# Three banks for transposed scores, three for projections, and the half-sums' addition one maximum later

## The chip, the cores and the metric

One core of a Trainium2 chip runs the kernel. The metric is the time of one execution on the device in microseconds (us). The engines have the profile's names: PE is TensorE (matmuls), PEld its loading of weights, DVE is VectorE, ACT is ScalarE, POOL is GpSimd, and SP issues the DMA transfers. TensorE writes its results to PSUM, which holds eight banks of 128 partitions x 512 fp32 values.

## The reference

Input x is 2048 tokens x 512. The result mixes an attention A and a gated layer B, token by token:

```python
g = sigmoid((x * gate_w).sum(-1, keepdims=True))
a = attention(x)      # 32 heads of 16; query q sees keys q-255 .. q; then @ wo
b = (sigmoid(x @ w_gate) * (x @ w_up)) @ w_down    # 512 -> 1376 -> 512
return g * a + (1 - g) * b
```

All of it is fp32 with random inputs. The kernel holds each factor of a large matmul as a high and a low part, so such a product is three matmuls.

## The kernel before

**Work in units.** The attention is cut into 128 units: 8 groups of 4 heads x 16 blocks of 128 tokens. The main loop (`for u in range(N)`, N = 140) does for each step u, and in it for each head hh of four:

- `s_part(u, hh)`, L306: the scores of a query block against its keys (a matmul to a PSUM bank of tag `s`), of which VectorE takes the row maximum at L312 (tile names `junk`, `mx`).
- `st_part(u - 9, hh)`, L353: the transposed scores of a unit nine steps back, with the maximum already taken off (a bank of tag `st`), of which ScalarE takes the exponential into a slot of `region` (L358). The unit's slot is u % 7 of seven slots of 1536 values.
- `run_slots(GAP)`: three slots of the projections, `gu` (the gated layer's two inputs) and `pj` (queries and keys of later groups), L238. Each group of 12 matmuls sums in one bank of tag `misc`, as two halves of 64 rows of the contraction, one on each half of the array; the second half runs 19 slots behind. When a group is done, ScalarE copies its bank out (`sp` at L494, `pr` at L250).
- Two lists of small jobs, `behind` (for VectorE, subtractions for low parts) and `acts` (for ScalarE): one job of each is popped per head, after that head's `s_part` and `st_part`.

**Bursts.** Every fourth step begins with a burst, `pv_burst` (L382): the exponentials of four query blocks times the values, small matmuls at L405, one half of the rows into a bank of tag `s` (`pvs`), the other into one of tag `st` (`pvst`). `o_take` adds the two half-sums: ScalarE copies `pvs` to `ob` (L419), VectorE adds `pvst` (L420). For the query blocks of units 120 to 127 the bursts are of two blocks.

**Banks.** The eight banks are two of tag `s`, two of tag `st` and four of tag `misc`. A tile takes the next bank of its tag in turn and waits until that one's last reader is done.

**Order.** Each engine runs its instructions in the order in which the code issues them; semaphores hold the engines together. So the order of the code around `s_part`, `st_part`, the pops and the slots is what sets the order of the work.

**Stages.** First the splits, the values and the first projections (to about 97 us); then the main loop with scores (to about 552 us); the tail, u from 128 to 139, with no scores left and six slots between its heads (to about 601 us); then the second phase: the gated layer's second matmul (`pd`, L77 to L79, in the four banks of tags `s` and `st`) and the attention's last projection (`pa`, tag `misc`). The gated layer's inputs went to DRAM as they were made (`gu_scratch`). `h_load(n)`, L567, loads step n's two raw pieces back into one of seven slots at the end of `region`, and `h_skew` turns them into the high and low parts `hb`, two or three steps ahead of `pd`. The loads of steps 0 to 4 are issued in the tail by the table HLOAD, at u = 135 (0), 136 (1), 137 (2 and 3) and 138 (4); from step 5 on, load n + 5 is issued in step n.

Of the kernel before, what the change touches and what calls it, by code (L numbers as in the profile page):

```python
# [7 lines left out]
F32 = mybir.dt.float32  # L8
# [25 lines left out]
REGION = PR * PW  # L34
NHV = 7
HV0 = REGION - NHV * 2 * CH
BURST = 4
# [17 lines left out]
def gated_mix_kernel(  # L55
# [70 lines left out]
    with ExitStack() as actx:  # L126
# [51 lines left out]
        nc.vector.memset(warm[:, 0:2 * P].bitcast(F32), 0.0)  # L178
        warm_ps = ps.tile([P, CH], F32, tag="st", name="warm_ps", bufs=2)
        for _ in range(16):  # L180
# [40 lines left out]
        def v_part(b, d):  # L221
            if d == 0:
                vp[b] = ps.tile([P, D], F32, tag="misc", name=f"vps{b}", bufs=4)
            bs = slice(b * P, (b + 1) * P)
            mm3(vp[b], xh[:, d, bs], xl[:, d, bs], wvh[:, d], wvl[:, d], d == 0, d == ND - 1)
            if d == ND - 1:
                nc.scalar.copy(Vh[:, b, :, 0:DH], vp.pop(b).rearrange("p (h w) -> p h w", w=DH))
                later.append((v_d[b], V[:, b]))
# [13 lines left out]
        def proj_mm(s, k, half=None):  # L242
            g, c = divmod(s, NC)
            if s not in pj:
                pj[s] = ps.tile([P, CH], F32, tag="misc", name=f"pj{s}", bufs=4)
            group_mm(pj[s], P, *wq[g], c, k, half)
# [49 lines left out]
        def s_part(u, hh):  # L296
# [5 lines left out]
            tag = "st" if u < LAG and hh >= 2 else "s"  # L302
            pt = ps.tile([P, 3 * P], F32, tag=tag, name=f"s{u}_{hh}", bufs=2)
            lhsT = blk(g, i, hh, 0)
# [39 lines left out]
        def st_part(u, hh):  # L344
            g, j = divmod(u, NB)
            if u not in pts:
                o = u % PR * PW
                pts[u] = region[:, o:o + PW].rearrange("p (h q) -> p h q", h=HG)
            pt = ps.tile([P, 3 * P], F32, tag="st", name=f"st{u}_{hh}", bufs=2)
            lhsT = blk(g, j, hh, 1)  # L350
# [32 lines left out]
        def pv_burst(u, n):  # L383
            g, i = divmod(u, NB)
            acc = [
                ps.tile([P, CH], F32, tag=tag, name=f"pv{tag}{u}", bufs=2) for tag in ("s", "st")
            ]
# [25 lines left out]
        def o_take(g, i, n, acc):  # L413
# [5 lines left out]
            nc.scalar.copy(part, acc[0][:, 0:n * P])  # L419
            nc.vector.tensor_tensor(part[:, lo:], acc[1][:, lo:n * P], part[:, lo:], op=ALU.add)  # L420
            if (i + n) % 4:
                return
            ob, c = obs.pop(s), i // 4
            for hh in range(HG):
                h = g * HG + hh
                later.append((oT_d[h * DH:(h + 1) * DH, c * CH:(c + 1) * CH], ob[32 * hh:32 * hh + DH]))
            later.append((sum_d[c, g * HG:(g + 1) * HG], ob.rearrange("(h r) f -> r h f", r=32)[DH]))

# [56 lines left out]
        def gu_mm(f, c, w, k, half=None):  # L485
            fw = width(f, w)
            if (f, c, w) not in gp:
                gp[f, c, w] = ps.tile([P, CH], F32, tag="misc", name=f"gu{f}_{c}_{w}", bufs=4)
            group_mm(gp[f, c, w], fw, gv[:, 0, w, :, 0:fw], gv[:, 1, w, :, 0:fw], c, k, half)
# [71 lines left out]
        steps = [(c, f) for c in range(NC) for f in range(NF)]  # L561
        hv = region[:, HV0:].rearrange("p (n w t) -> p n w t", w=2, t=CH)

        def h_load(n):
            c, f = steps[n]
            for w in range(2):
                nc.sync.dma_start(hv[0:FCH[f], n % NHV, w], gu_d[w, f, 0:FCH[f], c * CH:(c + 1) * CH])  # L567

        def h_skew(n):
            a, b = n + 2, n + 3  # L570
            if 0 <= a < len(steps):
                fw = FCH[steps[a][1]]
                hts[a] = cpool.tile([P, CH2], F32R, tag="hb", name=f"hb{a}", bufs=4)
                src = hv[0:fw, a % NHV, 1]
                split(hts[a][0:fw, 0:CH], hts[a][0:fw, CH:], src)
            if 0 <= b < len(steps):
                fw = FCH[steps[b][1]]
                tg, tu = hv[0:fw, b % NHV, 0], hv[0:fw, b % NHV, 1]
                nc.scalar.activation(tg, tg, AF.Sigmoid)
# [29 lines left out]
        U_LAST = 4 * (NSTEP - 2 - 5)  # L609
        HLOAD = {N - 5: [0], N - 4: [1], N - 3: [2, 3], N - 2: [4]}  # L610
        WD = NU - 5
# [10 lines left out]
        for u in range(N):  # L622
            if u == LAG:
                vctx.close()
                ppool = actx.enter_context(tc.tile_pool(name="ppool", bufs=1))
                for k in range(2):
                    vg.append(ppool.tile([P, NB * GW + 16], F32, name=f"vg{k}"))
                    nc.gpsimd.memset(vg[k][:, NB * GW:], 0.0)
            if u == LAG + 1 or u % NB == 0 and 0 < u < NU:
                v_load(u // NB)  # L630
# [69 lines left out]
            if SUMS + 2 <= u and (u - SUMS) % 4 == 2:  # L700
                behind.append(lambda c=(u - SUMS) // 4: later.append(sums_invert(c)))
            for n in HLOAD.get(u, ()):
                h_load(n)
            if u >= N - 2:
# [17 lines left out]
        def free_slot(h, d, c):  # L722
# [10 lines left out]
        spare = [  # L733
            region[:, 3 * CH * k:3 * CH * (k + 1)].rearrange("p (n t) -> p n t", t=CH) for k in range(2)
        ]
# [31 lines left out]
        for n, (c, f) in enumerate(steps):  # L767
# [10 lines left out]
            if f == 0:  # L778
                pd = [
                    ps.tile([P, D], F32, tag="s" if t < 2 else "st", name=f"pd{4 * c + t}", bufs=2)  # L780
                    for t in range(4)
# [25 lines left out]
            for t in range(4):  # L807
                b = 4 * c + t
                acc = accs[b % len(accs)]
                nc.scalar.activation(acc, pd[t], AF.Copy, scale=omg[:, b:b + 1])  # L810
                pa = ps.tile([P, D], F32, tag="misc", name=f"pa{b}", bufs=4)
                for d in range(ND):
# [57 lines left out]
```

## Time and profile before

| | us |
|---|---|
| median of three runs | 774.91 |
| the three runs | 773.41, 774.91, 775.33 |
| the profiled execution | 775.56 |
| its span in the trace | 773.9 |
| mean granted TensorE clock in it | 0.995 of full speed |

The runs and the profiled execution are times of whole executions; the trace's span runs from its first instruction to its last. In the views that follow, a group of rows has a line of the kernel, an engine, an operation and its tiles (`out<-in`); a wait's row says which engine and line waited for which other, how long in all, how often, and the longest. A row of the timeline is start, duration, engine, line, operation, tiles and shapes, and in brackets how long the engine stood idle before it and what ended that.

### The profile page before, as it was taken

To read this page: it belongs to the slowest core of one execution; us is meant where nothing else is said; L and a number is where in the kernel's file an instruction comes from. 1 tells how busy PE (TensorE), PEld (TensorE's weight loads), DVE (VectorE), ACT (ScalarE), POOL (GpSimd) and SP (SyncE) were. 2 spreads that over 40 slices of the span, in tenths; PEclk is the share of its full clock that TensorE was granted. 3 is DMA by queue.
4 is the path that set the end of the run, shared out by engine and by line. 5 is a ranking of instruction groups with operands and counts; after the bars stand their busy time and mean duration, and the time that the engine had idled before them with its cause. 6 is when DMAs were issued, how large, how long until landed. Compare 5 with 4: busy or idle time off the path is not lost.

```text
span 773.9 us, 20559 instructions
## 1 busy us (share of the span) xinstructions
PE 753.5 (97%) x7652; PEld 609.2 (79%) x7652; DVE 485.5 (63%) x1429; ACT 437.4 (57%) x900; POOL 163.4 (21%) x256
## 2 busy tenths in 40 slices
PE   8999999999999999999999999999999999999998
PEld 6877778877887877888787788888876778888886
DVE  5346767766676766766677676567511794839381
ACT  5412666666576656666667666665764663625341
POOL 7000323233133232323313323232331000000000
PEclk8999999999999999999999999999999999999999
DMA  8363544445444454444544425542346785648351
GB/s 292 97 207 130 142 130 127 121 108 160 120 125 116 123 146 133 116 109 123 149 130 113 127 68 158 150 143 79 111 128 206 230 275 192 212 147 258 105 165 54
DMA packets 88787, 112.69 MB, mean 146 GB/s; under 512 B 36082, under 2 KB 45810, under 8 KB 88688
## 3 DMA queue, kind: packets, MB, share of 16 engines
q1 hardware_dynamic: 88688, 111.39, 49.2%
q8 instruction: 60, 0.98, 0.5%
q14 instruction: 39, 0.32, 0.1%
HBM read 49.72 MB, written 36.45 MB: 111 GB/s over the span
## 4 chain that ended last, share of the span: by engine, by line
PE 84%; DVE 9%; DMA 3%; issue 2%; ACT 1%; SPq 1%; DVEq 0%; ACTq 0%
PE gu L238 32%; PE pvs L405 8%; PE pj L238 7%; PE s L306 6%; PE st L353 5%; PE pd L79 4%; PE pd L77 4%; PE pd L78 4%; DVE junk L312 3%; PE vps L77 2%; PE vps L78 2%; PE vps L79 2%; PE pa L77 2%; PE pa L79 2%; PE pa L78 2%
## 5 line engine op out<-in xcount | busy, mean ns | idle before, releaser
L238 PE MATMUL gu<-xh,w 64*128 64x512 f32 (+3 forms) x1384 | 357.3, 395 | 0.0
L312 DVE CUSTOM_DVE_ANT_0 junk<-s,mask 128x384 f32<-128x384 f32 (+2 forms) x512 | 271.1, 530 | 90.9 <-PE s L306 40.9
L358 ACT ACTIVATE region<-st 128x384 f32<-128x384 f32 (+2 forms) x512 | 238.6, 474 | 129.7 <-PE st L353 77.4
L238 PE MATMUL gu<-xl,w 64*128 64x512 f32 (+3 forms) x692 | 237.1, 394 | 0.0
L238 PEld LDWEIGHTS gu<-xh,w 64*128 64x128 f32 (+3 forms) x1384 | 206.5, 183 | 12.9 <-issue 0.2
L306 PE MATMUL s<-ring 64*128 64x384 f32 (+2 forms) x536 | 165.6, 333 | 9.8 <-DVE mx L312 9.5
L353 PE MATMUL st<-ring 64*128 64x384 f32 (+2 forms) x536 | 172.4, 338 | 2.1 <-DVE ob L420 1.3
L363 POOL TENSOR_SCALAR_AFFINE_SELECT region<-region 128x512 f32<-128x512 f32 x128 | 82.6, 646 | 368.2 <-ACT region L358 356.8
L306 PEld LDWEIGHTS s<-ring 64*128 64x128 f32 x536 | 94.1, 184 | 41.4 <-DVE mx L312 31.7
L238 PEld LDWEIGHTS gu<-xl,w 64*128 64x128 f32 (+3 forms) x692 | 116.8, 183 | 7.0 <-issue 1.6
L353 PEld LDWEIGHTS st<-ring 64*128 64x128 f32 x536 | 97.3, 184 | 18.1 <-DVE ob L420 11.7
L238 PE MATMUL pj<-xh,wqh 64*128 64x512 f32 (+1 forms) x232 | 94.4, 409 | 1.5 <-ACT xh L73 1.5
L238 PE MATMUL pj<-xl,wqh 64*128 64x512 f32 (+1 forms) x232 | 91.4, 398 | 0.4 <-DVE xl L74 0.2
L420 DVE TENSOR_TENSOR ob<-pvst,ob 128x512 f32<-128x512 f32 (+2 forms) x34 | 21.9, 645 | 100.9 <-ACT ob L419 82.8
L405 PE MATMUL pvs<-region,vg 64*32 64x320 f32 (+4 forms) x1440 | 74.5, 346 | 0.0
L238 PE MATMUL pj<-xh,wql 64*128 64x512 f32 (+1 forms) x232 | 73.2, 402 | 0.0
L405 PE MATMUL pvst<-region,vg 64*32 64x320 f32 (+4 forms) x1440 | 73.1, 341 | 0.0
L368 POOL TENSOR_SCALAR_AFFINE_SELECT region<-region 128x512 f32<-128x512 f32 x112 | 71.5, 638 | 0.0
L79 PE MATMUL pd<-ring,hb 128*128 128x512 f32 (+1 forms) x176 | 69.4, 394 | 0.9 <-DVE hb L74 0.9
L405 PEld LDWEIGHTS pvs<-region,vg 64*32 64x32 f32 x1440 | 49.7, 106 | 25.9 <-issue 9.5
L77 PE MATMUL pd<-ring,hb 128*128 128x512 f32 (+1 forms) x176 | 69.5, 395 | 0.3 <-ACT hb L73 0.3
L78 PE MATMUL pd<-ring,hb 128*128 128x512 f32 (+1 forms) x176 | 68.8, 391 | 0.4 <-DVE ring L119 0.4
(72 smaller groups left out, 1011.3 us busy)
## 6 DMA issues: line engine op xcount, KB each, us to landing
gu_scratch<-sp SPq DMA_DIRECT2D x80, 256.0 KB
region<-gu_scratch SPq DMA_DIRECT2D x80, 256.0 KB
ring<-sh SPq DMA_DIRECT2D x128, 128.0 KB
ring<-sl SPq DMA_DIRECT2D x64, 128.0 KB
guraw<-in_wgu_dram SPq DMA_DIRECT2D x20, 256.0 KB
v_scratch<-region SPq DMA_DIRECT2D x16, 272.0 KB
vg<-v_scratch SPq DMA_DIRECT2D x8, 544.0 KB
region<-in_xT_dram SPq DMA_DIRECT2D x16, 256.0 KB
```

Source lines behind the costliest of these rows:

```text
L77: mm(ps, lh, rh, start=first, stop=False)
L78: mm(ps, lh, rl, start=False, stop=False)
L79: mm(ps, ll, rh, start=False, stop=last)
L238: mm(pt[0:fw], (wl if w == 2 else wh)[r, d], (xl if w == 1 else xh)[r, d, c * CH:(c + 1) * CH], start=k == 0 and half != 1, stop=k == 3 * ...
L306: mm(pt[:, (k - k0) * P:(e - k0) * P], lhsT, blk(g, k, hh, 1, e - k), start=k == k0, stop=e == i + 1, skip_group_check=True,)
L312: nc.vector.tensor_tensor_reduce(junk[:, 0:n], pt[:, 0:n], mask[:, 3 * P - n:], scale=1.0, scalar=NEG, op0=ALU.add, op1=ALU.max, accum_out ...
L353: mm(pt[:, (q - j) * P:(e - j) * P], lhsT, blk(g, q, hh, 0, e - q), start=q == j, stop=e == last, skip_group_check=True,)
L358: nc.scalar.activation(pts[u][:, hh, 0:n], pt[:, 0:n], AF.Exp, scale=SCALE)
L363: nc.gpsimd.affine_select(p[:, :, 0:P], p[:, :, 0:P], pattern=[[0, HG], [1, P]], compare_op=ALU.is_ge, fill=0.0, base=0, channel_multiplie ...
L368: nc.gpsimd.affine_select(p[:, :, 2 * P:], p[:, :, 2 * P:], pattern=[[0, HG], [-1, P]], compare_op=ALU.is_gt, fill=0.0, base=0, channel_mu ...
L405: mm(acc[half][32 * hh:32 * hh + 32, q0:q1], vg[g % 2][r, c:c + 32], pts[g * NB + j][r, hh, q0 + o:q1 + o], start=m == 0, stop=m == len(or ...
L420: nc.vector.tensor_tensor(part[:, lo:], acc[1][:, lo:n * P], part[:, lo:], op=ALU.add)
```

## The change

**Banks.** Tag `st` has three banks, tag `misc` three, tag `s` two as before. The tiles of the start, `vps`, `pj`, `gu`, `pa`, `pd` and the warm-up are counted alike.

**The addition.** In `o_take`, VectorE's addition of `pvst` and the issue of the finished `ob` are put into a function `rest`, which goes to the front of `behind`. It is popped after the first head's `s_part` and `st_part` of the same step.

**Raw pieces.** The seven slots of the second phase's raw pieces are no longer the end of `region`: the first is the front of `vg0` (the values' buffer of the even groups), the others lie at six fixed places in `region` (HVO). The exponentials of the last seven units take slots 2, 3, 6, 0, 1, 2, 3 (PSLOT), so that they don't lie there. Loads 0 to 4 are issued at u = 130, 132, 134, 136 and 138. Buffers of the second phase that were at the front of `region` move by SPARE.

```diff
-NHV = 7
-HV0 = REGION - NHV * 2 * CH
+PSLOT = [w % PR for w in range(121)] + [2, 3, 6, 0, 1, 2, 3]
+HVO = [6144, 7168, 8192, 9216, 0, 1024]
+SPARE = 3072
+NHV = len(HVO) + 1
...
-                pj[s] = ps.tile([P, CH], F32, tag="misc", name=f"pj{s}", bufs=4)
+                pj[s] = ps.tile([P, CH], F32, tag="misc", name=f"pj{s}", bufs=3)
...
-            pt = ps.tile([P, 3 * P], F32, tag=tag, name=f"s{u}_{hh}", bufs=2)
+            pt = ps.tile([P, 3 * P], F32, tag=tag, name=f"s{u}_{hh}", bufs=2 if tag == "s" else 3)
...
-                o = u % PR * PW
+                o = PSLOT[u] * PW
...
-            pt = ps.tile([P, 3 * P], F32, tag="st", name=f"st{u}_{hh}", bufs=2)
+            pt = ps.tile([P, 3 * P], F32, tag="st", name=f"st{u}_{hh}", bufs=3)
...
-                ps.tile([P, CH], F32, tag=tag, name=f"pv{tag}{u}", bufs=2) for tag in ("s", "st")
+                ps.tile([P, CH], F32, tag=tag, name=f"pv{tag}{u}", bufs=bufs)
+                for tag, bufs in (("s", 2), ("st", 3))
...
             nc.scalar.copy(part, acc[0][:, 0:n * P])
-            nc.vector.tensor_tensor(part[:, lo:], acc[1][:, lo:n * P], part[:, lo:], op=ALU.add)
-            if (i + n) % 4:
-                return
-            ob, c = obs.pop(s), i // 4
...
+            def rest():
+                nc.vector.tensor_tensor(part[:, lo:], acc[1][:, lo:n * P], part[:, lo:], op=ALU.add)
+                if (i + n) % 4:
+                    return
+                ob, c = obs.pop(s), i // 4
...
+            behind.insert(0, rest)
...
-                gp[f, c, w] = ps.tile([P, CH], F32, tag="misc", name=f"gu{f}_{c}_{w}", bufs=4)
+                gp[f, c, w] = ps.tile([P, CH], F32, tag="misc", name=f"gu{f}_{c}_{w}", bufs=3)
...
-        HLOAD = {N - 5: [0], N - 4: [1], N - 3: [2, 3], N - 2: [4]}
+        HLOAD = N - 2 * AHEAD
...
+                hvs += [
+                    v.rearrange("p (w t) -> p w t", t=CH)
+                    for v in [vg[0][:, 0:2 * CH]] + [region[:, o:o + 2 * CH] for o in HVO]
+                ]
...
-            for n in HLOAD.get(u, ()):
-                h_load(n)
+            if u >= HLOAD and (u - HLOAD) % 2 == 0:
+                h_load((u - HLOAD) // 2)
...
-                    ps.tile([P, D], F32, tag="s" if t < 2 else "st", name=f"pd{4 * c + t}", bufs=2)
+                    ps.tile([P, D], F32, tag="s" if t < 2 else "st", name=f"pd{4 * c + t}", bufs=2 + t // 2)
...
-                pa = ps.tile([P, D], F32, tag="misc", name=f"pa{b}", bufs=4)
+                pa = ps.tile([P, D], F32, tag="misc", name=f"pa{b}", bufs=3)
```

VectorE's instructions around the burst of step 54 (its half-sums are `pvst40`, named for the first query block's unit), before; a `junk` row is the maximum of the score that it names:

```order
L312 ISA junk53_3_3970,mx13_3863<-s53_3_3968,mask_155 128x384
L312 ISA mx13_3863 128x1
L420 TENSOR_TENSOR ob10_4028<-pvst40_3979,ob10_4028 128x512
L312 ISA junk54_0_4037,mx13_3863<-s54_0_4035,mask_155 128x384
L312 ISA mx13_3863 128x1
L312 ISA junk54_1_4050,mx13_3863<-s54_1_4048,mask_155 128x384
```

The same place in the changed kernel:

```order
L314 ISA junk53_3_3970,mx13_3863<-s53_3_3968,mask_155 128x384
L314 ISA mx13_3863 128x1
L314 ISA junk54_0_4036,mx13_3863<-s54_0_4034,mask_155 128x384
L314 ISA mx13_3863 128x1
L425 TENSOR_TENSOR ob10_4028<-pvst40_3979,ob10_4028 128x512
L314 ISA junk54_1_4050,mx13_3863<-s54_1_4048,mask_155 128x384
```

The addition stands behind the first maximum of its step and not in front of it; nothing else on VectorE changes places.

TensorE's order is the same in both, but not what its instructions wait for. Behind the same burst, before, with the engine in brackets for which an instruction waits (`s54_1` is the second score of step 54, `st45_0` the second transposed score, `gu3_3_0`, `gu3_2_0` and `gu3_0_1` are projection groups):

```order
L353 MATMUL st45_0_4052<-ring_63 128x384 [waits DVE_49]
L238 MATMUL gu3_3_0_3961<-xl_71,w0_72 128x512
L238 MATMUL gu3_2_0_3901<-xh_70,w0_72 128x512
...
L306 MATMUL s54_3_4074<-ring_63 128x384 [waits DVE_49]
L353 MATMUL st45_2_4078<-ring_63 128x384 [waits Activation_49]
L238 MATMUL gu3_0_1_4081<-xh_70,w0_72 128x512
```

And in the changed kernel:

```order
L355 MATMUL st45_0_4052<-ring_63 128x384
L240 MATMUL gu3_3_0_3961<-xl_71,w0_72 128x512
L240 MATMUL gu3_2_0_3901<-xh_70,w0_72 128x512
...
L308 MATMUL s54_3_4074<-ring_63 128x384 [waits DVE_49]
L355 MATMUL st45_2_4078<-ring_63 128x384 [waits PE_49]
L240 MATMUL gu3_0_1_4081<-xh_70,w0_72 128x512 [waits Activation_49]
```

The second transposed score of the step no longer waits for VectorE, and a projection group's first matmul waits for ScalarE, which copies out the group three before it.

More of the change, by code (lines that the diff above doesn't have):

```diff
@@ L178, in gated_mix_kernel @@
         nc.vector.memset(warm[:, 0:2 * P].bitcast(F32), 0.0)
-        warm_ps = ps.tile([P, CH], F32, tag="st", name="warm_ps", bufs=2)
+        warm_ps = ps.tile([P, CH], F32, tag="st", name="warm_ps", bufs=3)
         for _ in range(16):
@@ L222, in v_part @@
             if d == 0:
-                vp[b] = ps.tile([P, D], F32, tag="misc", name=f"vps{b}", bufs=4)
+                vp[b] = ps.tile([P, D], F32, tag="misc", name=f"vps{b}", bufs=3)
             bs = slice(b * P, (b + 1) * P)
@@ L419, in o_take @@
             nc.scalar.copy(part, acc[0][:, 0:n * P])
-            nc.vector.tensor_tensor(part[:, lo:], acc[1][:, lo:n * P], part[:, lo:], op=ALU.add)
-            if (i + n) % 4:
-                return
-            ob, c = obs.pop(s), i // 4
[L424 to L427, printed above, removed]
+            def rest():
[3 more added lines that the diff above has]
+                ob, c = obs.pop(s), i // 4
+                for hh in range(HG):
+                    h = g * HG + hh
+                    later.append((oT_d[h * DH:(h + 1) * DH, c * CH:(c + 1) * CH], ob[32 * hh:32 * hh + DH]))
+                later.append((sum_d[c, g * HG:(g + 1) * HG], ob.rearrange("(h r) f -> r h f", r=32)[DH]))
+            behind.insert(0, rest)
         def proj(s):
@@ L561, in gated_mix_kernel @@
         steps = [(c, f) for c in range(NC) for f in range(NF)]
-        hv = region[:, HV0:].rearrange("p (n w t) -> p n w t", w=2, t=CH)
+        hvs = []
         def h_load(n):
@@ L566, in h_load @@
             for w in range(2):
-                nc.sync.dma_start(hv[0:FCH[f], n % NHV, w], gu_d[w, f, 0:FCH[f], c * CH:(c + 1) * CH])
+                nc.sync.dma_start(hvs[n % NHV][0:FCH[f], w], gu_d[w, f, 0:FCH[f], c * CH:(c + 1) * CH])
         def h_skew(n):
@@ L573, in h_skew @@
                 hts[a] = cpool.tile([P, CH2], F32R, tag="hb", name=f"hb{a}", bufs=4)
-                src = hv[0:fw, a % NHV, 1]
+                src = hvs[a % NHV][0:fw, 1]
                 split(hts[a][0:fw, 0:CH], hts[a][0:fw, CH:], src)
@@ L577, in h_skew @@
                 fw = FCH[steps[b][1]]
-                tg, tu = hv[0:fw, b % NHV, 0], hv[0:fw, b % NHV, 1]
+                tg, tu = hvs[b % NHV][0:fw, 0], hvs[b % NHV][0:fw, 1]
                 nc.scalar.activation(tg, tg, AF.Sigmoid)
@@ L733, in gated_mix_kernel @@
         spare = [
-            region[:, 3 * CH * k:3 * CH * (k + 1)].rearrange("p (n t) -> p n t", t=CH) for k in range(2)
+            region[:, SPARE + 3 * CH * k:SPARE + 3 * CH * (k + 1)].rearrange("p (n t) -> p n t", t=CH) for k in range(2)
         ]
```

## The prediction

> **What bounds the kernel now.** I read the page's busy times first, then the windows by stage, then the waits of the loop, then the timeline of single bursts (L382, one every four steps, about 16.2 us).
>
> The page's first part: engine, busy time, share of the span, instructions.
>
> ```profile
> PE 753.5 (97%) x7652; PEld 609.2 (79%) x7652; DVE 485.5 (63%) x1429; ACT 437.4 (57%) x900; POOL 163.4 (21%) x256
> ```
>
> The windows view for the main loop: its stretch, its length, then busy time of PE, PEld, DVE, ACT, POOL, the granted clock, the DMA share and GB/s.
>
> ```profile
> 97.00:548.00 451.00, 441.41 (x5758) 363.14 (x5758) 309.65 (x1057) 288.56 (x624) 130.22 (x210) 1.00 0.45 125
> ```
>
> TensorE lacks 451.0 - 441.4 = 9.6 us of a busy loop, at full clock. By that row it is the bound, and 9.6 us is about all that removed waits could give here. But TensorE works in two 64-row halves, and a stalled half is hidden while the other streams. The waits of the loop (97 to 552 us) show the stalls: engine, line, who is waited for, us in total, times, longest.
>
> ```profile
> PEld s L306 <- DVE mx L312: 30.3, 65, 1.3
> DVE junk L312 <- PE s L306: 28.4, 95, 0.6
> PEld st L353 <- DVE ob L420: 9.3, 29, 0.4
> PE s L306 <- DVE mx L312: 9.3, 24, 0.9
> ```
>
> The third row is what the change aims at: one wait per burst, 9.3 / 29 = 0.32 us each. The first is three times as large, and in the other direction: scores wait for VectorE to read the score before. So which of the two engines is late behind a burst? The timeline of VectorE in one period:
>
> ```profile
> 258.32 0.69 DVE L420 TENSOR_TENSOR ob<-pvst,ob 128x512 f32<-128x512 f32 x1 [2.45 <-ACT ob L419]
> 258.93 0.55 DVE L312 CUSTOM_DVE_ANT_0 junk<-s,mask 128x384 f32<-128x384 f32 x1
> 259.63 0.56 DVE L312 CUSTOM_DVE_ANT_0 junk<-s,mask 128x384 f32<-128x384 f32 x1
> 260.34 0.56 DVE L312 CUSTOM_DVE_ANT_0 junk<-s,mask 128x384 f32<-128x384 f32 x1
> 260.83 0.69 DVE L264 TENSOR_TENSOR sl<-pr,sh 128x512 fp32r<-128x512 f32 x1
> 261.43 0.55 DVE L312 CUSTOM_DVE_ANT_0 junk<-s,mask 128x384 f32<-128x384 f32 x1
> ...
> 262.84 0.56 DVE L312 CUSTOM_DVE_ANT_0 junk<-s,mask 128x384 f32<-128x384 f32 x1
> 263.60 0.56 DVE L312 CUSTOM_DVE_ANT_0 junk<-s,mask 128x384 f32<-128x384 f32 x1 [0.19 <-PE s L306]
> 264.34 0.56 DVE L312 CUSTOM_DVE_ANT_0 junk<-s,mask 128x384 f32<-128x384 f32 x1 [0.17 <-PE s L306]
> ```
>
> From the addition on, VectorE starts a maximum every 0.71 us (260.34 - 259.63) without a pause, and an addition between two costs 0.49 (260.34 to 260.83) and 0.60 (260.83 to 261.43). Real lateness shows only at 263.60, which is 263.60 - 262.84 - 0.71 = 0.05 late, and at 264.34, 0.03 late. Behind this burst TensorE costs VectorE 0.08 us, not 0.32. VectorE, 63% busy on the page, paces this stretch.
>
> **Part 1: the addition behind the next maximum, with a third st bank.** TensorE, a weight load and the release in the same place:
>
> ```profile
> 257.71 0.59 ACT L419 COPY ob<-pvs 128x512 f32<-128x512 f32 x1 [1.88 <-PE pvst L405]
> 258.15 0.33 PE L306 MATMUL s<-ring 64*128 64x384 f32 x1
> 258.79 0.33 PE L306 MATMUL s<-ring 64*128 64x384 f32 x1
> 259.07 0.18 PEld L353 LDWEIGHTS st<-ring 64*128 64x128 f32 x1 [0.32 <-DVE ob L420]
> 259.81 0.33 PE L306 MATMUL s<-ring 64*128 64x384 f32 x1
> 263.23 0.33 PE L306 MATMUL s<-ring 64*128 64x384 f32 x1
> ```
>
> Removed: the second st's load at 259.07 waits for the addition's end, 258.32 + 0.69 = 259.01, plus 0.06 to wake. With a third bank it needs no wait, since pvst's bank is not the next in turn: TensorE goes on 0.32 earlier there.
>
> Moved: the first score ends at 258.15 + 0.33 = 258.48, and a maximum starts 0.04 behind its score (263.23 + 0.33 = 263.56, then 263.60). So the first maximum starts at 258.52, the addition 0.49 behind it at 259.01, the second maximum 0.60 behind that at 259.61, where it stood at 259.63. Two operations change places in front of the same third: VectorE gains 0.02. The two instructions, their lengths and the queue behind them stay.
>
> Who is late next? The third score needs the first maximum's end to reuse its bank; before, 258.93 + 0.55 = 259.48, now 258.52 + 0.55 = 259.07. It stood at 259.81 and comes up to 0.32 earlier. The fourth needs the second maximum, which moves by 0.02 only. So TensorE's lead is caught at the fourth score, and what is left of it, 0.1 to 0.2, serves only to fill VectorE's later pauses: 0.08 + 0.02 = 0.10 us for this burst.
>
> Every second burst is followed by a step without the L264 addition, so VectorE reaches TensorE sooner. One of that kind:
>
> ```profile
> 274.42 0.69 DVE L420 TENSOR_TENSOR ob<-pvst,ob 128x512 f32<-128x512 f32 x1 [2.57 <-ACT ob L419]
> 277.15 0.56 DVE L312 CUSTOM_DVE_ANT_0 junk<-s,mask 128x384 f32<-128x384 f32 x1
> 278.02 0.56 DVE L312 CUSTOM_DVE_ANT_0 junk<-s,mask 128x384 f32<-128x384 f32 x1 [0.31 <-PE s L306]
> 278.76 0.56 DVE L312 CUSTOM_DVE_ANT_0 junk<-s,mask 128x384 f32<-128x384 f32 x1 [0.17 <-PE s L306]
> ```
>
> Here the pauses are 278.02 - 277.15 - 0.71 = 0.16 and 0.03, 0.19 in all; I take 0.16, since a lead of 0.1 to 0.2 does not fill them wholly. Mean of the kinds 0.13; 29 x 0.13 = 3.8 us. Lower bound: only the changed places, 29 x 0.02 = 0.6. Upper bound: the whole wait, 9.3.
>
> **Part 2: three banks for projections.** The group three before must now have been copied out when a group starts; before, the group four before. The copies of ScalarE and the first weight load of the third group behind, for the first and the last of 36 such starts in the loop that have under 0.4 us left (the others have more):
>
> ```profile
> 92.83 0.58 ACT L494 COPY sp<-gu 128x512 f32<-128x512 f32 x1
> 93.79 0.18 PEld L238 LDWEIGHTS gu<-xh,w 64*128 64x128 f32 x1
> ...
> 543.48 0.58 ACT L494 COPY sp<-gu 128x512 f32<-128x512 f32 x1
> 544.37 0.18 PEld L238 LDWEIGHTS gu<-xh,w 64*128 64x128 f32 x1
> ```
>
> Left: 93.79 - 93.41 = 0.38, and 544.37 - 544.06 = 0.31; minus 0.06 to wake, 0.25. TensorE's lead of up to 0.2 behind a burst eats most of it, but not all. So I take nothing in the loop; the cost if it is gone is the third rival.
>
> **The tail (u from 128 on, about 553 to 600 us)** has no scores; VectorE stands idle there, so what a st wait costs is TensorE's. The waits of that window, and a copy with the load of the third group behind it:
>
> ```profile
> PEld st L353 <- DVE ob L420: 2.4, 3, 1.0
> PEld st L353 <- ACT region L358: 1.2, 2, 0.7
> PE st L353 <- ACT region L358: 0.8, 2, 0.5
> 557.59 0.60 ACT L494 COPY sp<-gu 128x512 f32<-128x512 f32 x1
> 557.77 0.41 PEld L238 LDWEIGHTS gu<-xh,w 64*128 64x128 f32 x2
> 575.97 0.59 ACT L494 COPY sp<-gu 97x512 f32<-97x512 f32 x1
> 576.34 0.16 PEld L238 LDWEIGHTS gu<-xh,w 64*97 64x97 f32 x1
> ```
>
> Gone with the third st bank: 2.4, and of the two waits on the exponential the 0.8 that TensorE itself stands: 3.2 (bounds 2.4 and 3.6). Come in their place: the load at 557.77 must wait until 557.59 + 0.60 + 0.06 = 558.25, 0.48 us; that at 576.34 until 576.62, 0.28; between them lies one more, taken as the larger. 0.48 + 0.48 + 0.28 = 1.2, and I take 1.3 with a slot's rounding. Net -1.9 (bounds -2.4 and, if each stall is felt on both halves, 2 x 1.3 - 2.4 = +0.2).
>
> **Part 3: raw pieces in early free buffers.** Five loads of two DMAs each leave for u = 130 to 138 instead of 135 to 138, into vg0 and pieces of region that no later unit writes. SP issues them among the oT stores, the first four earlier than before, the fifth at the same step. The waits between 600 and 640 us show what they could save:
>
> ```profile
> PEld pd L79 <- DVE hb L74: 2.2, 3, 0.8
> PE pd L79 <- DVE hb L74: 0.9, 3, 0.4
> DVE region L580 <- DMA region<-gu_scratch: 2.1, 1, 2.1
> ```
>
> The one DMA wait belongs to the sixth load, which both kernels issue in the second phase. So I take 0; bounds -0.9, TensorE's share of its waits there, and +0.9, the same once more if a store is pushed behind a load.
>
> **Sum.** -3.8 - 1.9 + 0 = -5.7. The profiled execution took 775.56 us (span 773.9), 0.65 above the median of the runs shown, 774.91. 774.91 - 5.7 = 769.2 us.
>
> **Rivals.**
> First, TensorE really paces the loop and the whole wait comes back. For it: the row of 441.41 in 451.00. Against it: VectorE's row of maxima every 0.71 us. It gives 774.91 - 9.3 - 1.9 = 763.7 us. The Trainium skill, page "Perfetto Trace Analysis", section "Identifying the Most-Contended Engine", takes occupancy as a fair measure for VectorE; by that rule 63% would leave room and this rival would hold. The trace disagrees behind the bursts, where VectorE's pauses sum to 0.08. Chance 0.14.
>
> Second, the wait re-forms: TensorE, let past the st, waits at the third and fourth score for the maxima, the row of 30.3 us grows by what the row of 9.3 loses, and only the changed places are gained. 774.91 - 0.6 - 1.9 = 772.4, or if the tail's stalls eat its gain too, 774.3; about 773.5. The Trainium skill, page "Perfetto Trace Analysis", section "Optimization Strategy", reads bubbles that recur as a sign of too few buffers, which speaks against this rival; the trace shows the bubble at every burst, but not that it is TensorE's alone. Chance 0.18.
>
> Third, slower: with a third st bank TensorE runs one st further ahead of ScalarE, so ScalarE's copies come one exponential later against TensorE, 0.49 by this row:
>
> ```profile
> 258.61 0.49 ACT L358 ACTIVATE region<-st 128x384 f32<-128x384 f32 x1 [0.32 <-PE st L353]
> ```
>
> Then every one of the 36 starts is missed by 0.49 - 0.25 = 0.24: 8.6 us, and the loop's gain is spent in them. 774.91 + 8.6 - 1.9 = 781.6 without the loop's gain, 777.8 with it; about 780. It decides once the copies slip by 0.25 us. Against it: ScalarE is 57% busy on the page and waits for st before the exponential above. Chance 0.10.
>
> The forecast has 0.58.
>
> **How the numbers follow.** 769.2 us. The forecast's own bounds: -1.9 - 0.6 gives 772.4, -1.9 - 5.5 (0.19 a burst) gives 767.5. The range runs from 762.0, which takes in the first rival with the tail's and the second phase's lower bounds (763.7 - 0.5 - 0.9 = 762.3), to 774.0, most of the second. Left out are the third and the top of the second, some 0.15. A difference of 0.3%, 2.3 us, is about what a measurement can tell from no change. Faster: 0.58 + 0.14 = 0.72. Same: 0.18. Slower: 0.10.
>
> **What would show it.** Right: the row of st waiting for ob gone from loop and tail; the second maximum behind a burst still about 1.3 us behind the old addition's start; the row of scores waiting for maxima longer than 30.3 by a few us; three stalls of gu loads on ScalarE near 558, 568 and 576; a period shorter by about 0.13. Wrong: a period shorter by 0.3 (VectorE was not the pace), gu or pj loads waiting for ScalarE within the loop (the third rival), a second phase that starts as early but ends otherwise (part 3 was not neutral).

## The result and the profile after

The changed kernel takes 767.81 us (median) against 774.50 beside it: the ratio is 0.9907, interval 0.9883 to 0.9930. One of its four executions took 1829.77 us and belongs to a slow state; the median is 767.81 with or without it. In a second set it took 767.42 against 774.78, ratio 0.9912 (0.9897 to 0.9927).

The profiled execution after took 765.99 us with a span of 764.3, so 9.6 less than the span before. Not all of that is the change's. The windows view of the first projections, from 10 to 20 us, first before, with the granted clock third from the end of the row:

```profile
10.00:20.00 10.00, 10.00 (x33) 7.68 (x33) 6.55 (x10) 6.05 (x11) 4.65 (x3) 0.73 0.97 344
```

and after:

```profile
10.00:20.00 10.00, 10.00 (x43) 8.21 (x43) 6.00 (x9) 5.90 (x10) 4.69 (x3) 1.00 0.92 336
```

TensorE had 0.73 of its clock there in the execution before, all of it after. The first maximum came at 43.16 and 40.46 us, and over all profiled executions of this study at 40.1 to 43.2 without any order in the kernels: before, add and before_sl have the same code up to there and came at 43.16, 40.80 and 42.07. The granted clock is not the whole measure of it, since misc3's reads 1.00 in this stretch and its first maximum came at 42.12. So the two spans are compared stage by stage. Three marks serve: ScalarE's copy behind the first burst, the one behind the 29th, and the first `pd` matmul. From the timeline before:

```profile
96.97 0.59 ACT L419 COPY ob<-pvs 128x512 f32<-128x512 f32 x1 [1.42 <-PE pvs L405]
547.55 0.59 ACT L419 COPY ob<-pvs 128x512 f32<-128x512 f32 x1 [1.42 <-PE pvs L405]
601.89 0.40 PE L77 MATMUL pd<-ring,hb 128*128 128x512 f32 x1
```

and after:

```profile
94.28 0.59 ACT L422 COPY ob<-pvs 128x512 f32<-128x512 f32 x1 [1.42 <-PE pvs L408]
542.02 0.59 ACT L422 COPY ob<-pvs 128x512 f32<-128x512 f32 x1 [1.42 <-PE pvs L408]
593.25 0.40 PE L79 MATMUL pd<-ring,hb 128*128 128x512 f32 x1
```

The loop's 28 periods went from 450.58 to 447.74 us, -2.8; the tail, from the 29th copy to the first `pd`, from 54.34 to 51.23, -3.1. That is -5.9 where the forecast said -5.7, with less in the loop and more in the tail. The medians differ by 6.7 and 7.4 us in the two sets, which is more than the 5.9 and, in the second profiled execution, 5.4 of loop and tail; what makes up the rest is not shown.

The waits of the loop after (97 to 552 us), in the columns of the prediction:

```profile
PEld s L308 <- DVE mx L314: 43.7, 102, 1.4
DVE junk L314 <- PE s L308: 30.0, 61, 2.8
PE s L308 <- DVE mx L314: 9.1, 17, 1.0
```

The row of st waiting for `ob` (9.3 us before) is gone, and the scores' wait for the maxima grew from 30.3 to 43.7. TensorE still waits, one place later. A burst after, VectorE and ScalarE's copy, and two loads of TensorE:

```profile
255.19 0.59 ACT L422 COPY ob<-pvs 128x512 f32<-128x512 f32 x1 [1.88 <-PE pvst L408]
256.00 0.56 DVE L314 CUSTOM_DVE_ANT_0 junk<-s,mask 128x384 f32<-128x384 f32 x1 [2.65 <-PE st L355]
256.04 0.18 PEld L355 LDWEIGHTS st<-ring 64*128 64x128 f32 x1
256.49 0.69 DVE L425 TENSOR_TENSOR ob<-pvst,ob 128x512 f32<-128x512 f32 x1
256.68 0.18 PEld L308 LDWEIGHTS s<-ring 64*128 64x128 f32 x1
257.09 0.55 DVE L314 CUSTOM_DVE_ANT_0 junk<-s,mask 128x384 f32<-128x384 f32 x1
257.70 0.18 PEld L308 LDWEIGHTS s<-ring 64*128 64x128 f32 x1 [0.20 <-DVE mx L314]
257.79 0.56 DVE L314 CUSTOM_DVE_ANT_0 junk<-s,mask 128x384 f32<-128x384 f32 x1
```

Counted from the copy: the first maximum at 0.81, the addition at 1.30, the second maximum at 1.90 (before, 258.93, 258.32 and 259.63 less 257.71: 1.22, 0.61 and 1.92). The forecast's chain holds to 0.01 us. The second st loads at 0.85 instead of 1.36 and the third score at 1.49 instead of 1.88; the fourth, at 2.51, is caught by a maximum. The third score's load before, and the st matmul that the code issues behind that score:

```profile
259.59 0.18 PEld L306 LDWEIGHTS s<-ring 64*128 64x128 f32 x1
259.65 0.34 PE L353 MATMUL st<-ring 64*128 64x384 f32 x1
```

That st starts at 259.65 and the score itself at 259.81 (a row of the prediction), although the code issues them the other way round. By the code they lie on different halves of the array (heads 2 and 3), so an instruction of one half can start ahead of one of the other that was issued before it.

### The profile page after: what moved, and what is told of

The parts are those of the page before. It is cut to its first block, busy times and chain, and to the rows that moved or that the text cites. A ratio compares the mean times of both kernels' runs of the same rounds, so it can differ in the third digit from the quotient of the medians.

```text
span 764.3 us, 20558 instructions
## 1 busy us (share of the span) xinstructions
PE 745.9 (98%) x7652; PEld 592.4 (78%) x7652; DVE 483.6 (63%) x1429; ACT 434.9 (57%) x900; POOL 163.7 (21%) x256
## 4 chain that ended last, share of the span: by engine, by line
PE 81%; DVE 9%; DMA 4%; SPq 3%; issue 2%; ACT 1%; DVEq 0%; ACTq 0%
PE gu L240 29%; PE pvs L408 8%; PE pj L240 7%; PE s L308 7%; PE st L355 4%; PE pd L81 4%; PE pd L79 4%; PE pd L80 4%; DVE junk L314 4%; PE vps L79 2%; SPq L282 2%; PE vps L80 2%; PE vps L81 2%; PE pa L79 2%; PE pa L81 2%
## 5 line engine op out<-in xcount | busy, mean ns | idle before, releaser
L240 PE MATMUL gu<-xh,w 64*128 64x512 f32 (+3 forms) x1384 | 353.7, 394 | 0.4 <-ACT sp L501 0.3
L240 PE MATMUL gu<-xl,w 64*128 64x512 f32 (+3 forms) x692 | 243.8, 394 | 0.0
L240 PEld LDWEIGHTS gu<-xh,w 64*128 64x128 f32 (+3 forms) x1384 | 203.6, 183 | 16.6 <-ACT sp L501 1.4
L308 PE MATMUL s<-ring 64*128 64x384 f32 (+2 forms) x536 | 168.0, 338 | 10.7 <-DVE mx L314 9.3
L355 PE MATMUL st<-ring 64*128 64x384 f32 (+2 forms) x536 | 169.1, 334 | 0.0
L240 PEld LDWEIGHTS gu<-xl,w 64*128 64x128 f32 (+3 forms) x692 | 124.5, 183 | 9.7 <-issue 1.6
L355 PEld LDWEIGHTS st<-ring 64*128 64x128 f32 x536 | 94.7, 184 | 6.1
L501 ACT COPY sp<-gu 128x512 f32<-128x512 f32 (+2 forms) x88 | 51.3, 584 | 2.4 <-PE gu L240 2.4
```

What stands on the lines that cost most here:

```text
L240: mm(pt[0:fw], (wl if w == 2 else wh)[r, d], (xl if w == 1 else xh)[r, d, c * CH:(c + 1) * CH], start=k == 0 and half != 1, stop=k == 3 * ...
L308: mm(pt[:, (k - k0) * P:(e - k0) * P], lhsT, blk(g, k, hh, 1, e - k), start=k == k0, stop=e == i + 1, skip_group_check=True,)
L355: mm(pt[:, (q - j) * P:(e - j) * P], lhsT, blk(g, q, hh, 0, e - q), start=q == j, stop=e == last, skip_group_check=True,)
L501: nc.scalar.copy(t[0:width(f, w)], gp.pop((f, c, w))[0:width(f, w)])
```

## The experiments

Each was timed in five rounds beside the kernel before, and its ratio is to the runs of before in the same set. "Loop", "tail" and "pd to pa" are the stretches between the marks above and from the first `pd` to the first `pa`, in the profiled execution. "nm" is the sum over the loop's 28 steps of the chain on `nm` (from the start of its first operation, L322 in the kernel before, to the start of the transposition, L327); why it stands here is told under the second run of the changed kernel. That it may be taken off is seen in before, misc3 and raw: their loops differ by up to 1.02 us, and agree to 0.04 once it is off.

| kernel | median | ratio (interval) | loop | nm | loop - nm | tail | pd to pa |
|---|---|---|---|---|---|---|---|
| before | 774.50 | | 450.57 | 24.55 | 426.02 | 54.35 | 33.55 |
| changed | 767.81 | 0.9907 (0.9883-0.9930) | 447.74 | 25.21 | 422.53 | 51.23 | 32.61 |
| changed, again | 767.42 | 0.9912 (0.9897-0.9927) | 448.26 | 26.03 | 422.23 | 51.23 | 34.08 |
| misc3 | 774.76 | 1.0007 (0.9995-1.0020) | 451.15 | 25.13 | 426.02 | 54.31 | 34.33 |
| banks | 769.61 | 0.9945 (0.9927-0.9963) | 449.30 | 24.08 | 425.22 | 51.25 | 34.59 |
| add | 776.51 | 1.0028 (1.0015-1.0041) | 452.73 | 22.71 | 430.02 | 54.42 | 33.23 |
| raw | 773.59 | 0.9994 (0.9983-1.0005) | 450.13 | 24.07 | 426.06 | 54.38 | 33.73 |
| banks_add | 768.87 | 0.9945 (0.9926-0.9965) | 449.33 | 26.91 | 422.42 | 51.21 | 34.19 |
| no_add | 763.01 | 0.9864 (0.9844-0.9884) | 442.76 | 25.33 | 417.43 | 51.01 | 33.69 |
| copy_more | 778.40 | 1.0064 (1.0045-1.0083) | 458.19 | 24.82 | 433.37 | 51.61 | 33.19 |
| sl_pool | 760.86 | 0.9838 (0.9817-0.9858) | 441.16 | 23.17 | 417.99 | 51.23 | 33.35 |
| before_sl | 772.31 | 0.9969 (0.9958-0.9981) | 448.11 | 24.17 | 423.94 | 54.34 | 34.09 |
| nm_late | 760.70 | 0.9830 (0.9808-0.9853) | 436.57 | 14.09 | 422.48 | 51.20 | 34.16 |
| nm_late_sl | 753.44 | 0.9735 (0.9715-0.9754) | 431.45 | 14.47 | 416.98 | 51.19 | 32.54 |

### One part at a time

**misc3**: a bank less for the projections, nothing else.

```diff
-                pj[s] = ps.tile([P, CH], F32, tag="misc", name=f"pj{s}", bufs=4)
+                pj[s] = ps.tile([P, CH], F32, tag="misc", name=f"pj{s}", bufs=3)
...
-                gp[f, c, w] = ps.tile([P, CH], F32, tag="misc", name=f"gu{f}_{c}_{w}", bufs=4)
+                gp[f, c, w] = ps.tile([P, CH], F32, tag="misc", name=f"gu{f}_{c}_{w}", bufs=3)
```

(and the same for `vps` and `pa`)

> The kernel before with three banks of tag misc and nothing else changed (one bank of PSUM is left unused). Theory (VectorE paces the loop, projection starts have about 0.25 us left): loop unchanged within 1 us, tail longer by 0.3 to 1.2 us through three starts that now wait for ScalarE's copy; 774.5 to 776. Rival (the starts in the loop are missed by 0.24 us, 36 of them): the loop longer by some 8 us, 782 to 784.

Measured: 774.76 us, the ratio's interval holds 1. Loop less nm 426.02, to the hundredth that of before, and the tail 54.31 against 54.35. The rival falls: no start in the loop is missed. But the tail did not lose the 0.3 to 1.2 us either. The copy and the loads at the first of the three places, in misc3:

```profile
557.13 0.59 ACT L494 COPY sp<-gu 128x512 f32<-128x512 f32 x1
557.31 0.41 PEld L353 LDWEIGHTS st<-ring 64*128 64x128 f32 x2
557.77 0.18 PEld L238 LDWEIGHTS gu<-xh,w 64*128 64x128 f32 x1
```

The group's load, at 557.77 in the kernel before where the copy began 0.46 later, waits here for the copy's end (557.72 + 0.05), 0.46 us later against the rest of its stretch, and the tail is as long as before. The stall is on one half of the array. The st loads beside it come in time (557.31, and 557.77 less 0.46 in the kernel before), and some 2 us further on the two kernels' loads are level again (559.91, and 560.41 less 0.46).

**banks**: three banks for st and three for misc; the addition and the raw pieces as before.

```diff
-            pt = ps.tile([P, 3 * P], F32, tag="st", name=f"st{u}_{hh}", bufs=2)
+            pt = ps.tile([P, 3 * P], F32, tag="st", name=f"st{u}_{hh}", bufs=3)
...
-                ps.tile([P, CH], F32, tag=tag, name=f"pv{tag}{u}", bufs=2) for tag in ("s", "st")
+                ps.tile([P, CH], F32, tag=tag, name=f"pv{tag}{u}", bufs=bufs)
+                for tag, bufs in (("s", 2), ("st", 3))
```

(with misc3's lines)

> The kernel before with three banks for st and three for misc; the addition and the raw pieces as before. Theory: the second st behind a burst finds a bank that is not pvst's, so its wait on the addition is gone without the addition being moved; the loop gains 2.0 to 2.8 us of the 2.8 measured, the tail most of its 3.1; about 769 to 770. Rival (the addition's new place makes the gain): loop gains under 1 us, 771.5 to 773.5.

Measured: 769.61 us, and the tail has its whole gain, 51.25. The time lies in the theory's range. The loop gained 1.3, between the two expectations; less nm it is 0.8, so for the loop the rival's figure is the right one. A burst in banks:

```profile
256.87 0.59 ACT L420 COPY ob<-pvs 128x512 f32<-128x512 f32 x1 [1.87 <-PE pvst L406]
257.73 0.18 PEld L353 LDWEIGHTS st<-ring 64*128 64x128 f32 x1
258.10 0.55 DVE L312 CUSTOM_DVE_ANT_0 junk<-s,mask 128x384 f32<-128x384 f32 x1
258.71 0.18 PEld L306 LDWEIGHTS s<-ring 64*128 64x128 f32 x1 [0.39 <-DVE mx L312]
```

The second st loads 0.86 behind the copy, as in the changed kernel. But the first maximum still comes behind the addition, at 1.23, and the third score waits for its bank until 1.84 (before 1.88, changed 1.49). A wait of 0.32 us on st became one of 0.39 on the next score.

**add**: the addition behind the next maximum, with two, two and four banks.

```diff
-            nc.vector.tensor_tensor(part[:, lo:], acc[1][:, lo:n * P], part[:, lo:], op=ALU.add)
+            def rest():
+                nc.vector.tensor_tensor(part[:, lo:], acc[1][:, lo:n * P], part[:, lo:], op=ALU.add)
...
+            behind.insert(0, rest)
```

> The kernel before with the addition behind the next maximum only; banks two, two and four. Theory: the second st needs pvst's bank, free only at 259.70 in place of 259.01 behind the burst at 257.71, and the third score stands behind that st, so the third maximum starts about 0.5 us late: 29 x 0.5 = 15 us longer in the loop, 785 to 791. Rival (VectorE's run behind the burst hides it, or the other half covers it): within 3 us of 774.5.

Measured: 776.51 us, slower, but the loop by 2.2 (4.0 less nm) and not 15; that is in the rival's range. The expectation had the second st take `pvst`'s bank. The timeline says otherwise:

```profile
257.15 0.49 ACT L358 ACTIVATE region<-st 128x384 f32<-128x384 f32 x1 [0.31 <-PE st L353]
257.54 0.69 DVE L422 TENSOR_TENSOR ob<-pvst,ob 128x512 f32<-128x512 f32 x1
257.69 0.18 PEld L353 LDWEIGHTS st<-ring 64*128 64x128 f32 x1 [0.41 <-ACT region L358]
262.24 0.56 DVE L312 CUSTOM_DVE_ANT_0 junk<-s,mask 128x384 f32<-128x384 f32 x1 [0.29 <-PE s L306]
```

It waits for the exponential of the first st (257.64) and starts before the addition ends. The loop's waits of add (97 to 552 us) show the same 28 times, and no st waiting for `ob`:

```profile
PEld st L353 <- ACT region L358: 12.1, 28, 0.7
```

So the banks do not go in turn, though the part on the kernel says so. What fits is that a tile takes the bank whose last reader was issued first, and here the exponential is issued ahead of the moved addition; no other run tests it. The st loads 1.44 us behind the copy (256.25) where it was 1.36, and TensorE stays later: the seventh maximum, which waits for its score, starts at 5.99 where it was 5.89 (263.60 less 257.71). 4.0 us in 28 periods are 0.14 each.

**raw**: the early raw pieces alone, on the kernel before.

```diff
-HV0 = REGION - NHV * 2 * CH
+PSLOT = [w % PR for w in range(121)] + [2, 3, 6, 0, 1, 2, 3]
+HVO = [6144, 7168, 8192, 9216, 0, 1024]
...
-        HLOAD = {N - 5: [0], N - 4: [1], N - 3: [2, 3], N - 2: [4]}
+        HLOAD = N - 2 * AHEAD
```

(with what belongs to them in `h_load`, `h_skew` and `spare`)

> The kernel before with the early raw pieces only. Theory: loop and tail unchanged within 0.5 us; the stretch from the first pd to the first pa, 33.55 us before and 32.62 after the change, gains 0 to 0.9; 773.5 to 774.7. Rival (the tail's surplus of some 1.2 us over the forecast comes from the loads): the tail shorter by 1 us or more, 772.5 to 773.3.

Measured: 773.59 us, ratio 0.9994 with 1 in its interval; loop less nm 426.06, tail 54.38. Neither loop nor tail moves. From the first `pd` to the first `pa` it took 33.73; see banks_add.

**banks_add**: the changed kernel without the raw pieces.

```diff
-        HLOAD = N - 2 * AHEAD
+        HLOAD = {N - 5: [0], N - 4: [1], N - 3: [2, 3], N - 2: [4]}
```

(and raw's other lines taken back)

> The changed kernel without the early raw pieces. Theory: loop and tail as changed; the stretch from the first pd to the first pa loses up to 0.9 us of its gain; 767.8 to 768.8. Rival (the raw pieces carry a part of the tail's gain): 769 or more.

Measured: 768.87 us, between the two ranges, ratio 0.9945. The tail is the changed kernel's, which ends the rival. Loop less nm, 422.42, is too. The loop itself, 449.33, is longer by its nm chains. From `pd` to `pa` it took 34.19. Over all executions that stretch takes 32.5 to 34.2 with the raw pieces (eight, mean 33.4) and 33.2 to 34.6 without (six, mean 34.0): the sets overlap, and what the raw pieces are worth stays open, between nothing and about 1 us in these profiles. The ratios, 0.9907 and 0.9912 with them and 0.9945 without, would allow more; they were taken in different sets.

### Who paces the loop

**no_add**: the changed kernel without the addition; the attention's output lacks one half-sum.

```diff
             def rest():
-                nc.vector.tensor_tensor(part[:, lo:], acc[1][:, lo:n * P], part[:, lo:], op=ALU.add)
                 if (i + n) % 4:
```

> The changed kernel without VectorE's addition of pvst: the attention's output lacks one half-sum, everything else is computed. Theory (VectorE paces the loop): VectorE has 0.60 us less behind each burst, 29 x 0.60 = 17 us, of which TensorE's own load lets pass at most its idle time in the loop, 451.0 - 440.5 = 10.5; loop shorter by 3 to 9 us, 759 to 765. Rival (TensorE paces it): loop the same within 1 us, 767 to 768.5.

**copy_more**: one more copy on VectorE behind each addition.

```diff
                 nc.vector.tensor_tensor(part[:, lo:], acc[1][:, lo:n * P], part[:, lo:], op=ALU.add)
+                more = spool.tile([P, 3 * P], F32, tag="more", name=f"more{g}_{i}", bufs=1)
+                nc.vector.tensor_copy(more[:, 0:min(3, n) * P], part[:, 0:3 * P] if n == 4 else part[:, 0:2 * P])
```

> The changed kernel with one more operation on VectorE behind each burst's addition, a copy of up to 384 columns of ob to a spare tile, of 0.2 to 0.6 us. Theory: VectorE has no slack behind a burst, so the loop is longer by most of it: 29 x 0.2 to 0.5 = 6 to 15 us, 773 to 783. Rival (TensorE paces): hidden, under 1.5 us longer, 767.5 to 769.5.

Measured: 763.01 and 778.40 us. The copy, in the groups by line:

```profile
L427 DVE COPY more<-ob 128x384 f32<-128x384 f32 (+1 forms) x34 | 12.0, 353 | 1.2
```

The loop less nm grew by 433.37 - 422.4 = 11.0 us, 0.39 in each of 28 periods: all of the copy's 0.36 and a little more. Without the addition it fell by 5.0, 0.18 a period of the 0.60 freed. So VectorE has no slack behind a burst; that with 0.60 taken away TensorE becomes the later after a third of it is the likely reading of the second figure. "TensorE paces" falls by both.

**sl_pool** and **before_sl**: the loop's subtractions `sl` on GpSimd, in the changed kernel and in the one before.

```diff
-        def proj_lo(s):
+        def proj_lo(s, eng=nc.vector):
...
-            nc.vector.tensor_tensor(sl, pj.pop(s), sh.bitcast(F32), op=ALU.subtract)
+            eng.tensor_tensor(sl, pj.pop(s), sh.bitcast(F32), op=ALU.subtract)
...
-            acts.append(lambda: (proj_hi(s), behind.append(lambda: proj_lo(s))))
+            acts.append(lambda: (proj_hi(s), behind.append(lambda: proj_lo(s, nc.gpsimd))))
```

> The changed kernel with the loop's subtractions sl (low parts of the projections, 0.60 us of VectorE between two maxima, about 26 of them) moved to GpSimd. Theory: VectorE is relieved by 26 x 0.60 = 16 us, of which TensorE lets pass a part; loop shorter by 2 to 6 us, 762 to 766, if GpSimd, 21% busy, has the low parts ready in time. Rival (TensorE paces): the same within 1.5 us, or slower if the later low parts hold up the ring's transfers.

> The kernel before with the loop's subtractions sl moved to GpSimd, as they were in the changed kernel's version at 760.86 us. Theory (what the change is worth depends on who paces): with VectorE relieved, TensorE paces more of the loop and its wait on the addition, 0.32 a burst, counts more nearly whole; the loop is 5 to 9 us longer than the 441.2 of that version, the tail 3.1, so 769 to 773. Rival (the change gives its 2.8 us in the loop whoever paces): loop 444.0, 766.5 to 767.5.

Measured: 760.86 us, more of a gain than the 762 to 766 expected, and 772.31 us, as expected. Moving `sl` takes 6.6 us off the changed kernel's loop and only 2.5 off the loop before (less nm 4.5 and 2.1). With `sl` on VectorE the change is worth 2.3 to 2.8 us in the loop, with `sl` on GpSimd 448.11 - 441.16 = 6.95; less nm, the fairer measure, it is 3.5 to 3.8 and 423.94 - 417.99 = 5.95. That is the theory's 5 to 9 and not the rival's 2.8. In before_sl the wait is still there, as large as ever:

```profile
PEld st L353 <- DVE ob L420: 9.5, 29, 0.4
```

Less nm, the same wait costs some two fifths of its length while VectorE paces, and nearly two thirds of it when VectorE has been relieved.

### The second run, and the chain on nm

**after_again**: the changed kernel itself, with no edit.

> The changed kernel once more. Theory: the loop of another profiled execution differs from the first one's 447.7 us only in periods in which VectorE's operations on nm, behind the maxima of every fourth step, start beside GpSimd's select or just before it: steps of about 0.5 us, so 446.5 to 449.5, and each longer period holds a longer nm chain; time 766.5 to 769. Rival (the early raw pieces shorten the loop, since without them it took 449.3): loop again at 447.7 within 0.2, with the same nm chains.

Measured: 767.42 us, loop 448.26. Most of its periods agree with the first execution's to 0.05 us. Three don't: the 6th is 0.55 shorter, the 14th and the 20th are 0.54 and 0.51 longer, and in each the nm chain differs by 0.55. The theory's reading holds: banks_add's 449.33 was such steps, not the missing raw pieces. What such a step is, in the timeline of VectorE and GpSimd of the changed kernel's first execution:

```profile
278.14 0.17 DVE L324 TENSOR_SCALAR nm<-mx 128x16 fp32r<-128x16 f32 x1
278.14 0.67 POOL L365 TENSOR_SCALAR_AFFINE_SELECT region<-region 128x512 f32<-128x512 f32 x1 [2.26 <-ACT region L360]
278.35 0.49 DVE L325 SCALAR_TENSOR_TENSOR nm<-mx,nm 128x16 fp32r<-128x16 f32 x1
278.87 0.21 DVE L329 STREAM_TRANSPOSE nt<-nm 128x32 f32<-128x32 f32 x1
```

and of the same period in banks_add:

```profile
280.02 0.64 POOL L363 TENSOR_SCALAR_AFFINE_SELECT region<-region 128x512 f32<-128x512 f32 x1 [2.25 <-ACT region L358]
280.03 0.66 DVE L322 TENSOR_SCALAR nm<-mx 128x16 fp32r<-128x16 f32 x1
280.61 0.64 POOL L368 TENSOR_SCALAR_AFFINE_SELECT region<-region 128x512 f32<-128x512 f32 x1
280.73 0.55 DVE L323 SCALAR_TENSOR_TENSOR nm<-mx,nm 128x16 fp32r<-128x16 f32 x1
```

An operation on 16 columns takes 0.17 us when it starts level with GpSimd's select and 0.66 when it starts 0.01 behind it. Then the next one meets the second select. The chain is 0.73 us in the one, 1.28 in the other. This holds for every operation on `nm` in the changed kernel's first execution: 40 of the 64 take over 0.3 us, each of these starts while a select runs and ends 0.02 to 0.03 us behind that select, and the other 24 start while none runs.

**nm_late**: the three operations two maxima later, with their store, and the load that follows one step later.

```diff
-            if u % 4 == 3 and u < NU:
-                max_split(u // 4)
+            if u % 4 == 3 and u < NU:
+                behind[0:0] = [lambda: None, lambda s=u // 4: (max_split(s), max_store(s))]
...
-            if u % 4 == 0 and 0 < u <= NU:
-                max_store(u // 4 - 1)
...
-            if u % 4 == 1 and 1 < u <= NU + 1:
+            if u % 4 == 2 and 2 < u <= NU + 2:
                 max_load(u // 4 - 1)
```

> The changed kernel with the nm operations of every fourth step two maxima later (and their store and load with them), so that they no longer start with GpSimd's select. Theory: the chain on nm falls from 0.73 to 1.28 us to about 0.42, and VectorE, which paces, gives the most of it back: 28 x 0.2 to 0.4; loop shorter by 4 to 8 us, 760 to 764. Rival (the chain is long by itself, or the wait is for something else than the select): chain as before, loop within 1 us.

**nm_late_sl**: this and `sl` on GpSimd.

> Both: the nm operations later, and the subtractions sl on GpSimd. Theory: TensorE's load bounds the loop now; it took 440.5 us of busy time within 451.0, so the loop's 28 periods come to 436 to 440 us and the time to 755 to 760. Rival (VectorE paces on): the two gains add up whole, 6.6 and 4 to 8, loop under 436.

Measured: 760.70 and 753.44 us. The chain in nm_late where no select runs:

```profile
261.90 0.17 DVE L324 TENSOR_SCALAR nm<-mx 128x16 fp32r<-128x16 f32 x1
262.11 0.18 DVE L325 SCALAR_TENSOR_TENSOR nm<-mx,nm 128x16 fp32r<-128x16 f32 x1
262.32 0.21 DVE L329 STREAM_TRANSPOSE nt<-nm 128x32 f32<-128x32 f32 x1
```

0.42 us; with the steps that still meet a select the mean is 0.50 (14.09 / 28). The chains fell from 25.2 to 14.1, and the loop by as much, 11.2: less nm it is 422.48, the changed kernel's. More than the 4 to 8 expected, since the whole of it came back. The scores' wait for the maxima halved, in the loop's waits of nm_late:

```profile
PEld s L308 <- DVE mx L314: 21.8, 76, 0.5
```

Ahead of the loop's first burst nm_late loses 1.75 us (from the first maximum 55.57 against 53.82), where the first st now wait for the later load; in its waits over the whole span:

```profile
PE st L355 <- DMA ring<-max_scratch: 5.6, 5, 1.8
```

The longest of the five, 1.8, is the one ahead of that burst; the other four lie in the loop.

nm_late_sl has the two gains nearly whole: 431.45 where 447.74 - 11.2 - 6.6 would be 429.9; that is the rival's loop under 436. The bound that the expectation took from TensorE's busy time, 436 to 440, falls. That busy time was no fixed load: in the windows view it was 440.47 us for 5786 matmuls in the changed kernel (97 to 548 us), and is 428.78 for 5785 in nm_late_sl (97 to 530). That a half which waits is counted as busy while the other streams is the likely reason, and not shown. nm_late_sl is the fastest of all, 2.65% under the kernel before (interval 2.46 to 2.85).

## Why the prediction came out as it did

**What paces the loop: right.** VectorE paces it at 63% busy; a copy of 0.36 us behind a burst lengthened each period by 0.39, and 11.1 us less of `nm` shortened the loop by 11.2. Much of VectorE's idle time lies where it has nothing to do, during the burst itself; in the loop's waits of the kernel before (97 to 552 us):

```profile
DVE ob L420 <- ACT ob L419: 62.7, 27, 2.6
```

That is 2.3 us a burst, and no slack for what stands behind it. The rule of the Trainium skill, page "Perfetto Trace Analysis", section "Identifying the Most-Contended Engine", on which the first rival could rest (occupancy as a fair measure for VectorE), would leave room for that copy; copy_more disagrees.

**The loop's term: right in mechanism and size, with something on top.** The forecast was 0.13 a period, 3.8 us in all. Less nm, the loop fell by 3.5 and 3.8 us in two executions. The step "who is late next" is what the two parts show apart: the third bank alone gives TensorE nothing at the third score (1.84 against 1.88) and 0.8 us in the loop, the moved addition alone makes it 4.0 us longer less nm, the two together give the 3.6. The raw loop gained only 2.8 and 2.3, since the nm chains came out 0.7 and 1.5 us longer. The prediction quoted no row of `nm` and did not have this. The mean of 0.13 was taken from two bursts; the 28 periods, less nm, run from 0.11 longer to 0.45 shorter, so that it came out to the hundredth is partly luck.

**The tail: mis-sized.** "Net -1.9" was 3.2 off for the st waits and 1.3 on for three projection starts. The tail fell by 3.1: the first term was right and the second cost nothing. The three stalls are there, in the tail's waits of the changed kernel (545 to 600 us), first on the loads and then on TensorE:

```profile
PEld gu L240 <- ACT sp L501: 1.4, 3, 0.7
PE gu L240 <- ACT sp L501: 0.3, 1, 0.3
```

1.4 us, near the 1.2 worked out, but TensorE as a whole stood only 0.3 of it, and misc3 shows that the tail does not lengthen by it. The prediction let a stall of one half count as TensorE's, against its own opening remark on halves. The st waits counted almost in full, 3.1 of the 3.6 that the loads stood. In the tail's waits of the kernel before (553 to 600 us) there is this row, which the prediction left out:

```profile
PE st L353 <- DVE ob L420: 1.3, 3, 0.6
```

With the 0.8 behind the exponential, TensorE as a whole stood 2.1 us in the st waits, against 0.3 in the projection starts. That goes the right way, but leaves 1.0 of the 3.1; that ScalarE's and the next burst's work hangs on the st is argued, not shown.

**The projections' banks in the loop: right.** misc3's loop less nm is that of before to 0.01; the third rival's price was not due. In the changed kernel's loop one start waits for ScalarE, 0.2 us.

**The raw pieces: taken at nothing**, and not told apart from it: raw gives 0.9994 (0.9983 to 1.0005).

**The sum: partly luck.** -5.7 stands against -5.9 because two errors cancel: the tail gave 1.2 us more than forecast, and the loop 1.0 less.

**The rivals.** The first needed the whole 0.32 a burst; 0.13 came. With `sl` on GpSimd it would have been nearer the truth (0.21, less nm). The second has the right picture in banks, where the wait did re-form a place later (0.39 on the third score).

## What to carry to other kernels

Before a wait is priced, ask which engine is late behind it: the same 0.32 us per burst was worth 0.13 while VectorE paced and 0.21 once it was relieved (less nm), so here a removed wait and a relieved engine gave more together, 8.0 us, than the two apart, 2.1 and 3.5 to 3.8. A single bank or a single reordering may give almost nothing where both together do, because the next resource in the chain is one instruction further; follow the release chain until it meets an instruction that did not move. Find the operations on the pacing engine whose length varies for no reason of their own: here moving three tiny ones by two places took 11.2 us off the loop where the change took 2.3 to 2.8, and, with what it lost ahead of the loop, about as much off the whole time (6.7 us and 7.4, in the same set).

## What the runs showed of the hardware

**Two engines in each other's way.** VectorE's operation on 128 x 16 values took 0.17 or 0.66 us, its follower 0.18 or 0.55, by whether GpSimd's select on `region` had begun; in the rows shown, which of them is first is decided within 0.01 us, so the same program has periods that differ by 0.55 from one execution to the next. The Trainium skill, page "SBUF — State Buffer", section "Who interferes with whom", has such a rule: a VectorE operation in a two-port mode contends with GpSimd for a pair of ports that the two share, one with two inputs in SBUF contends with a GpSimd operation that reads SBUF, and whichever is issued first blocks the other for its whole length. The rows agree in both directions of it that they show: the select first (0.66), the scalar operation first (0.17, and the next, with two inputs, 0.49). That the scalar operation runs in a two-port mode is not shown by any run. nm_late, which moves the operations away from the select, has 0.42 for the chain where none runs.

**The banks of a tag do not go in turn.** In add the second st took the first st's bank, whose reader was issued ahead of the addition, and loaded 0.08 us later, not 0.69. This is the order in which the program hands out banks, and nothing of the chip's.

**The first matmuls** start 0.43 us or more apart in every profiled execution, and 0.23 apart from some point on; that point is 15.5 us in the execution before, ahead of 11.7 in the one after, and 13.9 in misc3. The granted clock tells of it in the first two, 0.73 and 1.00 from 10 to 20 us, but not in misc3, where it reads 1.00. The first maxima of before and after lie 2.7 us apart, and those of before and add, with the same code up to there, 2.4.
